# Keeping three quarters, not two, of one weight granule in PSUM, with attention sums and turned tiles in other banks

## The chip, the cores and the metric

One core of one Trainium2 chip runs the kernel. The metric is the device time of one execution in microseconds (us), lower being better. Three plain executions of the kernel before and one profiled execution are known.

## The reference

The reference normalises a bf16 sequence `x` of 2048 rows and 1024 columns and sends it through a recurrent attention layer with memory and through a layer that handles two routed rows. Cut to what matters here:

```
xn = layernorm(x)
mem = mem0                                  # 8 rows x 1024
for s in range(64):                         # segments of 32 rows
    h = concat(mem, xn[32*s : 32*s+32])     # 40 rows
    q, k, v = h @ Wq, h @ Wk, h @ Wv        # 32 heads x 128
    p = softmax(mask(q @ k.T / sqrt(128)))
    o = (p @ v) @ Wo                        # 40 x 1024
    mem = o[:8]                             # carried on
    outs.append(o[8:])
y = gate/up/down on the two rows of xn with the largest xn @ w_r
out = x + concat(outs) + xn, plus y * sigmoid(r) added at the two rows
```

Every segment needs the memory that the one before it made, so the 64 segments run one after the other, and each of them uses all four weight matrices (32 MiB in bf16).

## The kernel before

**Weights.** The matrices are cut into 64 granules of 128 partitions by 2048 bf16 columns, 512 KiB each: granules 0 to 47 are the halves of Wq, Wk and Wv in the order of the six phases (eight granules to a phase: q first half, k first half, q second half, k second half, v first half, v second half), and 48 to 63 are Wo. Of these, 44 stay in SBUF for the whole run. The other 20 (the list `STREAMED`) are used in every segment and are streamed: `fetch` (L366) loads each into one of five slots of the pool `wstream` (tile `g`), from copies `wsc` in DRAM that segment 0 makes. A slot is reloaded when TensorE has used its granule for the last time in the segment; the load is issued by SP, whose queue is in program order, so the loads come in the order of use.

**What of the streamed granules stays in PSUM.** Two streamed granules are kept in PSUM too. Granule 6 (`KEPT_WHOLE`) is kept whole, in the tiles KEPT0 and KEPT1, and never loaded after segment 0; ScalarE and VectorE copy its four quarters (512 columns each) to SBUF in each segment (`bring_back`, L389). Of granule 25 (`KEPT_PART`, the second granule of the fourth phase) the last two quarters are kept, in KEPT2. In each segment from 1 on, `fetch` loads its first 1024 columns (256 KiB), and VectorE copies the other two quarters from KEPT2 into the same slot (`kept_piece`, L393). In segment 0, `keep` (L377 to L382) brings a quarter to PSUM: four transposes on TensorE into the tile BT, a copy to SBUF on VectorE (XK, L380), and four transposes back into the KEPT tile.

**A segment.** For a granule, TensorE makes four matmuls (L817) of the segment's 32 rows (24 new rows and 8 rows of memory, tile ST) into an accumulator PSm. The eight new rows that each segment leaves out of ST are gathered over four segments and projected for four segments at once (`left_pass`, L579, tile STL; `project_left`, L598). ScalarE empties the accumulators (XB, L836; VM, L846). Half a phase later, XB is turned by four transposes (L649) into BT and copied out as QT (ScalarE, L657) or KT (VectorE, L664); next to the first QT also the left rows LX are turned (L502) and copied as QKL (ScalarE, L506). Then follow the scores in the tile BS (L672, L674), the softmax on VectorE and ScalarE (L681 to L720), the attention sums (`attend`, L736 and L738), which are copied as OT and OTL (L745, L747), and the product with Wo (L586) into WO. In the midst of that product, at its ninth granule, the next segment's rows XN are turned (L301) and copied to the next ST (L315). The memory rows come last: X (L885), turned (L301) and copied to ST by VectorE (L324).

**Banks.** BS and BT are one PSUM bank each (128 partitions by 512 f32 columns). Before the change BT holds turned tiles in its first half (`PTB`) and, in its second half, the turned LX (`PTB2`) or half of the attention sums (`OPB`). BS holds the scores (columns 0 to 319), the other half of the sums of the second half of heads, and row statistics from column 320 on. The order of instructions is the one in which the code is written, with hooks at (phase, granule); waits are set between any two engines that use one bank, whichever columns they use.

Of the kernel before, what the change touches and what calls it, by code (L numbers as in the profile page):

```python
# [8 lines left out]
BF16 = mybir.dt.bfloat16  # L9
# [11 lines left out]
KEPT_PART = 25  # L21
# [29 lines left out]
def kernel(  # L51
# [16 lines left out]
    nc = tc.nc  # L68
# [9 lines left out]
    NT = S // P  # L78
# [6 lines left out]
    NK = M + SEG  # L85
# [43 lines left out]
    def columns(g, s):  # L129
        if s > 0 and g == KEPT_WHOLE:  # L130
            return None
        return slice(0, 1024 if s > 0 and g == KEPT_PART else 2048)

    wsc = {g: dram.tile([P, columns(g, 1).stop - columns(g, 1).start], BF16, name=f"wsc{g}")
           for g in streamed if g != KEPT_WHOLE}
# [24 lines left out]
    BS = psS.tile([P, 512], F32, name="BS")  # L160
    BT = psT.tile([P, 512], F32, name="BT")
    SPS = BS[:, 0:8 * NK].rearrange("p (i a k) -> p i a k", i=4, a=2)
    PTB = BT[:, 0:256].bitcast(BF16)
    PTB2 = BT[:, 256:512].bitcast(BF16)
    OPB = BT[:, 256:256 + 4 * NK]
    MR = BS[:, 320:320 + 2 * NSEG].rearrange("p (s c) -> p s c", c=2)
    ML = BS[:, 448:448 + 2 * NT].rearrange("p (t c) -> p t c", c=2)
    MLR = BS[:, 480:480 + 2 * NT].rearrange("p (t c) -> p t c", c=2)
# [30 lines left out]
    for s in range(4):  # L199
        nc.vector.tensor_copy(out=SELM[:, s, :, 0:XM],  # L200
                              in_=IDENT[:, 32 * s:32 * s + XM].unsqueeze(1).to_broadcast([P, 4, XM]))
        nc.vector.tensor_copy(out=SELL[:, s, :, :],
                              in_=IDENT.rearrange("p (s c) -> p s c", c=32)[:, :, XM:SEG])
        nc.vector.tensor_copy(out=SELR[:, s, :, :],
                              in_=IDENT.rearrange("p (s c) -> p c s", c=32)[:, XM:SEG, :])
# [78 lines left out]
    def norm_seg(s):  # L284

        x = X[s % 2]
        mr = two_rows(MR[:, s, :], "ri")
        ab = mr[:, 2:4]
        nc.vector.tensor_scalar(out=ab[:, 0:1], in0=mr[:, 1:2], scalar1=1.0, scalar2=KMSK, op0=ALU.add, op1=ALU.mult)
        nc.vector.tensor_scalar(out=ab[:, 1:2], in0=mr[:, 0:1], scalar1=mr[:, 1:2], scalar2=-1.0, op0=ALU.mult, op1=ALU.mult)  # L290
        xn = front.tile([P, 256], BF16, tag="st", name="XN")
        nc.vector.tensor_scalar(out=xn[:, :], in0=x[:, :], scalar1=mr[:, 0:1], scalar2=mr[:, 1:2],
                                op0=ALU.subtract, op1=ALU.mult)
        nc.vector.tensor_scalar(out=x[:, :], in0=x[:, :], scalar1=ab[:, 0:1], scalar2=ab[:, 1:2],
                                op0=ALU.mult, op1=ALU.add)
        return xn

    def turn(src, at=0):
        PTx = PTB[:, 256 * at:256 * (at + 1)].rearrange("p (c g r) -> p c g r", c=2, g=4)
        for c in range(2):  # L300
            nc.tensor.transpose(out=PTx[:, c, :, :].rearrange("p g r -> p (g r)"), in_=src[:, c * P:(c + 1) * P],  # L301
                                identity=IDENT[:, :])
        return PTx
# [1 line left out]
    def gview(st):  # L305
        return st.rearrange("p (g c) r -> p c g r", c=2)

    def turn_rows(xn, xl):

        return turn(xn), turn(xl, 1) if xl is not None else None  # L310

    def new_st(turned):
        PTx, PTl = turned
        st = front.tile([P, KC, SEG], BF16, tag="st", name="ST")
        nc.scalar.copy(out=gview(st)[:, :, :, 0:XM], in_=PTx[:, :, :, 0:XM])  # L315
        if PTl is None:
            return st, None
        stl = one.tile([P, KC, SEG], BF16, tag="stl", name="STL")
        nc.scalar.copy(out=gview(stl), in_=PTl[:, :, :, :])
        return st, stl  # L320

    def mem_to_st(OB, st):
        PTm = turn(OB)
# [17 lines left out]
    def sum_left(t, G):  # L341
# [10 lines left out]

    KEPT = [psK.tile([P, 1024], BF16, name=f"KEPT{b}") for b in range(3)]
    KEPT_COLS = {KEPT_WHOLE: {0: KEPT[0][:, 0:512], 1: KEPT[0][:, 512:1024], 2: KEPT[1][:, 0:512], 3: KEPT[1][:, 512:1024]},
                 KEPT_PART: {2: KEPT[2][:, 0:512], 3: KEPT[2][:, 512:1024]}}

    def fetch():
        if not flow:
# [14 lines left out]
    def keep(g, t):  # L373
        for c, K in KEPT_COLS[g].items():
            turned = PTB.rearrange("p (i r) -> p i r", i=4)
            for i in range(4):
                nc.tensor.transpose(out=turned[:, i, :], in_=t[:, 512 * c + P * i:512 * c + P * (i + 1)],  # L377
                                    identity=IDENT[:, :])
            XK = one.tile([P, 512], BF16, tag="vl0", name="XK")
            nc.vector.tensor_copy(out=XK[:, :], in_=PTB)  # L380
            for i in range(4):
                nc.tensor.transpose(out=K[:, P * i:P * (i + 1)], in_=XK[:, P * i:P * (i + 1)], identity=IDENT[:, :])  # L382

# [7 lines left out]
    def kept_piece(g, c, copy):  # L391
        t = [t for q, t in queued if q == g][0]
        copy(out=t[:, 512 * c:512 * (c + 1)], in_=KEPT_COLS[g][c])  # L393
# [30 lines left out]
    def granule(g):  # L424
        if g in res_tiles:
            return res_tiles[g]
        got, t = queued.pop(0)
        assert got == g, (got, g)
        return t
# [26 lines left out]
    row_stats(xt(0), S6, MV[:, 0, :])  # L456
    spread(0, 1)
    norm_left(XL0, 0)
    ST, STL = new_st(turn_rows(norm_seg(0), XL0))
    mem_to_st(OB, ST)  # L460

    side = {}
# [34 lines left out]
    lx = [None]  # L497

    def turn_lx():
        PTq = PTB2.rearrange("p (i c) -> p i c", i=4)  # L500
        for il in range(4):
            nc.tensor.transpose(out=PTq[:, il, :], in_=lx[0][:, il * P:(il + 1) * P], identity=IDENT[:, :])  # L502

    def new_qkl():
        t = qkl[0] = one.tile([P, 4, 4, 4, XL], BF16, tag="bC", name="QKL")
        nc.scalar.copy(out=t.rearrange("p i m q r -> p (i m q r)"), in_=PTB2)  # L506

    def turn_first(mat, half, XBl):
        if mat == 0 and half == 0:
# [122 lines left out]
    for s in range(NSEG):  # L632
# [10 lines left out]
        def hook(p, kc, fn):  # L643
            hooks.setdefault((p, kc), []).append(fn)
# [79 lines left out]
        def attend(half, ph, turn_too=None):  # L724
            if half not in sums:
                if half not in OT:
                    OT[half] = one.tile([P, 4, 4, SEG], BF16, tag=("kt", "bC")[half], name="OT")
                if half == 0:
                    nxt["wo"] = psA.tile([P, 512], F32, tag="acc", name="WO")
                sums[half] = [BS[:, 0:4 * NK] if half else nxt["wo"][:, 256:256 + 4 * NK], OPB]  # L730
            PTm, PTl = PTs[half]
            for il in range(4):
                for jl in range(2):
                    q0 = 32 * (2 * ph + jl)
                    o = sums[half][jl][:, il * NK:(il + 1) * NK]
                    nc.tensor.matmul(o, lhsT=VM[half][q0:q0 + 32, il * P:(il + 1) * P], rhs=PTm[q0:q0 + 32, il, 0:NK],  # L736
                                     start=True, stop=False, tile_position=(q0, 0), skip_group_check=True)
                    nc.tensor.matmul(o, lhsT=VL[half][q0:q0 + 32, il * P:(il + 1) * P], rhs=PTl[q0:q0 + 32, il, 0:NK],  # L738
                                     start=False, stop=True, tile_position=(q0, 0), skip_group_check=True)
            if turn_too is not None:  # L740
                turn_too()
            for jl in range(2):
                ov = sums[half][jl].rearrange("p (i q) -> p i q", i=4)
                copy = nc.scalar.copy if half == 0 or jl == 0 else nc.vector.tensor_copy
                copy(out=OT[half][:, 2 * ph + jl, :, :], in_=ov[:, :, 0:SEG])  # L745
                h0 = 16 * half + 8 * ph + 4 * jl
                copy(out=left_out()[:, h0:h0 + 4, j, :], in_=ov[:, :, SEG:NK])  # L747
# [42 lines left out]
        if s > 0:  # L790
            hook(0, 0, lambda: bring_back(3, nc.scalar.copy))
            hook(0, 1, lambda: bring_back(0, nc.vector.tensor_copy))
            hook(2, 1, lambda: kept_piece(KEPT_PART, 2, nc.vector.tensor_copy))
            hook(2, 2, lambda: kept_piece(KEPT_PART, 3, nc.vector.tensor_copy))
        hook(2, 6, lambda: scores(0))
        hook(3, 4, exponent)
        hook(3, 4, lambda: soften(0))
# [54 lines left out]
        assert not hooks, hooks  # L852

        WO = nxt["wo"]
        if s + 1 < NSEG:
            xn = norm_seg(s + 1)
            left_too = nxt["xl"] if j == 0 and G + 1 < NT else None
            turned = []

        def lhs_main(h):  # L860
# [3 lines left out]
        for w in range(16):  # L864
            if w == 5:
                attend(1, 0)
            if w == 8 and s + 1 < NSEG:
                attend(1, 1, lambda: turned.append(turn_rows(xn, left_too)))
                nxt["st"], stl = new_st(turned[0])
                STL = stl or STL  # L870
            elif w == 8:
                attend(1, 1)
            Gv = granule(48 + w)
            project(WO, w, Gv, lhs_main, w == 15, first=(w == 0))
            held[48 + w] = Gv
            run_passes(6, w)
            if w == 9 and s + 1 < NSEG:
                new_lx(s + 1)
                bring_back(1, nc.scalar.copy)
                bring_back(2, nc.vector.tensor_copy)  # L880
            if w == 11 and j == 3:
                xl_of[0] = load_left(G, one.tile([P, 256], BF16, tag="stl", name="OL")[:, :], True)
            release(6, w)
# [129 lines left out]
```

## Time and profile before

| what | value |
|---|---|
| three executions | 1874.32, 1879.33, 1879.33 us (median 1879.33) |
| the profiled execution's own time | 1871.24 us |
| its span, first to last instruction | 1869.5 us |
| PE busy, DVE busy, ACT busy, POOL busy | 84%, 47%, 37%, 24% of the span |
| moved by DMA | 712.27 MB, mean 381 GB/s |
| granted TensorE clock, mean | 0.956 |

PE is TensorE's matmul row, PEld its weight loads, DVE VectorE, ACT ScalarE, POOL GpSimd and SP the engine that issues the loads. In the groups of instructions a row is: line, engine, operation, out<-in, shapes, count, then busy time, mean ns of one, and idle time before them with what ended it. In the waits a row is: who waited, for whom, us in total, times, longest. In the table by stretches the last two columns are the mean busy share of the 16 DMA engines (packets overlap a little, so that it can pass 1.00) and GB/s. Segment 0, with the first loads of all weights, takes the time up to about 131 us; the last segment begins at about 1784 us.

### The profile page before, as it was taken

The page shows a single profiled execution, that of the slowest core. Times are in us where ns is not written, and L with a number is a line of the kernel's source. Part 1 is how long each engine was busy: PE and PEld are TensorE (multiplying, and loading weights), DVE is VectorE, ACT ScalarE, POOL GpSimd, SP SyncE. Part 2 cuts the span into 40 slices and gives each one's busy share as a digit, 9 for nine tenths or more (in the row PEclk, how much of TensorE's full clock was granted, in tenths as well). Part 3 has the DMA queues.
Part 4 walks back from the last instruction along what each step waited for, and adds up shares of the span by engine and source line. Part 5 has one row for each costly group of instructions (what it writes and reads, how often), then busy time and mean ns, then how long its engine had stood idle before and what let it go on. Part 6 is the DMA issues. An engine that isn't in the chain of part 4 may idle for free.

```text
span 1869.5 us, 80499 instructions
## 1 busy us (share of the span) xinstructions
PE 1565.6 (84%) x34978; PEld 851.4 (46%) x34978; DVE 886.3 (47%) x2935; ACT 692.7 (37%) x1948; POOL 455.8 (24%) x898
## 2 busy tenths in 40 slices
PE   3458998898888989988899889988898888888764
PEld 1124444444454544444445444444444444444433
DVE  6725544544454454444444454444544454445430
ACT  1113433444343334433443344433433343434320
POOL 3211322213131321323132221323132121312120
PEclk8669999999999999999999999999999999999995
DMA  9999999999999999999999999999999999999998
GB/s 371 399 358 391 382 367 391 390 370 369 379 381 379 376 374 388 382 390 373 388 384 400 379 391 385 379 398 375 392 368 382 380 385 390 379 395 380 374 403 325
DMA packets 232115, 712.27 MB, mean 381 GB/s; under 512 B 39040, under 2 KB 52912, under 8 KB 231760
## 3 DMA queue, kind: packets, MB, share of 16 engines
q1 hardware_dynamic: 194384, 671.18, 93.0%
q0 software_dynamic: 28736, 28.08, 4.7%
q10 hardware_dynamic: 8640, 7.87, 1.2%
q8 instruction: 274, 4.49, 0.9%
q14 instruction: 81, 0.66, 0.1%
HBM read 694.32 MB, written 22.29 MB: 383 GB/s over the span
## 4 chain that ended last, share of the span: by engine, by line
DMA 58%; PE 35%; DVE 4%; issue 2%; SPq 1%; ACT 1%; POOL 0%; DVEq 0%; POOLq 0%; ACTq 0%
DMA g<-wsc 50%; PE PSm L817 18%; PE WO L586 5%; PE PSl L579 4%; PE BT L649 2%; DMA XP<-in_A_x_dram 2%; PE WL L598 2%; DMA MW<-in_B_w_up_dram 1%; DVE XR L256 1%; DMA MW<-in_B_w_gate_dram 1%; DMA g<-in_A_Wq_dram 1%; DMA wres<-in_A_Wo_dram 1%; DMA g<-in_B_w_down_dram 1%; PE BT L301 1%; DMA out_dram<-X 1%
## 5 line engine op out<-in xcount | busy, mean ns | idle before, releaser
L817 PE MATMUL PSm<-wres,ST 128*32 128x512 bf16 x8448 | 702.2, 383 | 9.1 <-DMA wres<-in_A_Wv_dram 4.1
L817 PEld LDWEIGHTS <-ST 128*32 128x32 bf16 x12288 | 322.4, 96 | 411.2 <-issue 163.8
L817 PE MATMUL PSm<-g,ST 128*32 128x512 bf16 x3588 | 359.8, 385 | 100.0 <-DMA g<-wsc 77.0
L586 PEld LDWEIGHTS <-OT 128*32 128x32 bf16 x8192 | 219.9, 98 | 157.3 <-issue 130.5
L836 ACT CAST XB<-PSm 128x512 bf16<-128x512 f32 x256 | 150.5, 588 | 283.8 <-PE PSm L817 281.3
L586 PE MATMUL WO<-wres,OT 128*32 128x256 bf16 x5632 | 240.8, 281 | 13.9 <-DMA wres<-in_A_Wo_dram 7.5
L495 POOL DMA_DIRECT2D LX<-ql_d x63 | 35.3, 560 | 819.6 <-PE WO L586 380.6
L586 PE MATMUL WO<-g,OT 128*32 128x256 bf16 x2560 | 133.8, 283 | 76.5 <-DMA g<-wsc 66.3
L579 PE MATMUL PSl<-wres,STL 128*32 128x512 bf16 x2112 | 185.9, 390 | 1.6 <-issue 1.5
L664 DVE COPY KT<-BT 128x512 bf16<-128x512 bf16 x112 | 45.8, 409 | 290.7 <-issue 177.4
L887 POOL DMA_DIRECT2D out_dram<-X x256 | 129.8, 514 | 199.6 <-DVE X L885 158.6
L281 POOL DMA_DIRECT2D X<-in_A_x_dram x256 | 129.7, 513 | 188.3 <-PE PSm L817 88.7
L657 ACT COPY QT<-BT 128x512 bf16<-128x512 bf16 x128 | 75.0, 586 | 125.4 <-PE BT L502 73.6
L389 ACT COPY BK<-KEPT 128x512 bf16<-128x512 bf16 x126 | 74.4, 590 | 120.7 <-PE WO L586 93.2
L649 PEld LDWEIGHTS <-XB 128*128 128x128 bf16 x1024 | 58.4, 98 | 117.1 <-ACT XB L836 65.5
L579 PEld LDWEIGHTS <-STL 128*32 128x32 bf16 x3072 | 84.5, 98 | 57.3 <-issue 11.9
L649 PE MATMUL BT<-IDENT,XB 128*128 128x128 bf16 x1024 | 101.8, 222 | 8.7 <-ACT XB L836 7.3
L846 ACT CAST VM<-PSm 128x512 bf16<-128x512 f32 x128 | 76.0, 594 | 84.4 <-PE PSm L817 82.9
L736 PEld LDWEIGHTS <-VM 32*128 32x128 bf16 x2048 | 66.4, 91 | 84.8 <-issue 70.0
L885 DVE TENSOR_TENSOR X<-WO,X 128x256 bf16<-128x256 f32 x64 | 27.1, 424 | 160.9 <-PE WO L586 160.9
L745 DVE CAST OT<-BT 128x128 bf16<-128x128 f32 x128 | 37.2, 291 | 126.7 <-PE BT L301 71.6
L745 ACT CAST OT<-BS 128x128 bf16<-128x128 f32 x128 | 34.1, 266 | 166.0 <-PE BT L738 89.7
(175 smaller groups left out, 2406.9 us busy)
## 6 DMA issues: line engine op xcount, KB each, us to landing
g<-wsc SPq DMA_DIRECT2D x1134, 512.0 KB, 6.1
g<-wsc SPq DMA_DIRECT2D x63, 256.0 KB, 5.6
LX<-ql_d POOLq DMA_DIRECT2D x63, 128.0 KB, 5.8
ql_d<-XBl ACTq DMA_DIRECT2D x60, 128.0 KB, 5.8
MW<-in_B_w_gate_dram SPq DMA_DIRECT2D x16, 448.0 KB, 9.1
MW<-in_B_w_up_dram SPq DMA_DIRECT2D x16, 448.0 KB, 9.4
wres<-in_A_Wk_dram SPq DMA_DIRECT2D x12, 512.0 KB, 11.9
MW<-in_B_w_down_dram SPq DMA_DIRECT2D x12, 512.0 KB, 10.5
```

What stands on the lines that cost most here:

```text
L281: nc.gpsimd.dma_start(out=X[s % 2][32 * g:32 * g + XM, :], in_=x2[s * SEG:s * SEG + XM, 256 * g:256 * (g + 1)])
L389: copy(out=back[c][:, :], in_=KEPT_COLS[KEPT_WHOLE][c])
L579: nc.tensor.matmul(PSl[32 * jq:32 * jq + 32, :], lhsT=STL[:, g % KC, :], rhs=part(Gv, jq), start=first_, stop=last_, tile_position=(0, 32 ...
L586: nc.tensor.matmul(PS[32 * g:32 * g + 32, 0:256], lhsT=lhs(h), rhs=Gv[:, D * hs + 256 * g:D * hs + 256 * (g + 1)], start=(first and hs == ...
L649: nc.tensor.transpose(out=PTq[:, il, :, :].rearrange("p j r -> p (j r)"), in_=XB[:, il * P:(il + 1) * P], identity=IDENT[:, :])
L657: nc.scalar.copy(out=QT[half][:, :, :], in_=pv)
L736: nc.tensor.matmul(o, lhsT=VM[half][q0:q0 + 32, il * P:(il + 1) * P], rhs=PTm[q0:q0 + 32, il, 0:NK], start=True, stop=False, tile_position ...
L745: copy(out=OT[half][:, 2 * ph + jl, :, :], in_=ov[:, :, 0:SEG])
L817: nc.tensor.matmul(PSm[32 * jq:32 * jq + 32, :], lhsT=ST[:, kc, :], rhs=part(Gv, jq), start=(kc == 0), stop=(kc == KC - 1), tile_position= ...
L836: nc.scalar.copy(out=XB[:, :], in_=PSm[:, :])
L846: nc.scalar.copy(out=VM[half][:, :], in_=PSm[:, :])
L887: nc.gpsimd.dma_start(out=out2[s * SEG:s * SEG + XM, 256 * g:256 * (g + 1)], in_=OB[32 * g:32 * g + XM, :])
```

## The change

Three of granule 25's quarters are kept, and the load of that granule in segments 1 to 63 shrinks from 256 to 128 KiB (1024 bytes of each partition). The third quarter lies in BT's second half, so what lay there moves: the sums `OPB` to BT's first half, the turned LX to BS (`PTS`), and the turned XN to columns 160 to 287 of BS. The left rows of the next group (`left_too`, one segment in four) are turned into BT on their own, at the thirteenth granule of Wo rather than the ninth. `kept_piece` runs three times per segment, at hooks (2, 0) to (2, 2), and XK in segment 0 is copied by ScalarE.

```diff
-        return slice(0, 1024 if s > 0 and g == KEPT_PART else 2048)
+        return slice(0, 512 if s > 0 and g == KEPT_PART else 2048)
...
-    PTB2 = BT[:, 256:512].bitcast(BF16)
-    OPB = BT[:, 256:256 + 4 * NK]
+    PTS = BS[:, 0:256].bitcast(BF16)
+    OPB = BT[:, 0:4 * NK]
...
-                 KEPT_PART: {2: KEPT[2][:, 0:512], 3: KEPT[2][:, 512:1024]}}
+                 KEPT_PART: {1: BT[:, 256:512].bitcast(BF16), 2: KEPT[2][:, 0:512], 3: KEPT[2][:, 512:1024]}}
...
-            nc.vector.tensor_copy(out=XK[:, :], in_=PTB)
+            nc.scalar.copy(out=XK[:, :], in_=PTB)
...
-        PTq = PTB2.rearrange("p (i c) -> p i c", i=4)
+        PTq = PTS.rearrange("p (i c) -> p i c", i=4)
...
-        nc.scalar.copy(out=t.rearrange("p i m q r -> p (i m q r)"), in_=PTB2)
+        nc.scalar.copy(out=t.rearrange("p i m q r -> p (i m q r)"), in_=PTS)
...
-            hook(2, 1, lambda: kept_piece(KEPT_PART, 2, nc.vector.tensor_copy))
-            hook(2, 2, lambda: kept_piece(KEPT_PART, 3, nc.vector.tensor_copy))
+            for c in range(1, 4):
+                hook(2, c - 1, lambda c=c: kept_piece(KEPT_PART, c, nc.vector.tensor_copy))
...
             if w == 8 and s + 1 < NSEG:
-                attend(1, 1, lambda: turned.append(turn_rows(xn, left_too)))
-                nxt["st"], stl = new_st(turned[0])
-                STL = stl or STL
+                attend(1, 1, lambda: turned.append(turn(xn, BS[:, 160:288].bitcast(BF16))))
+                nxt["st"] = new_st(turned[0])
             elif w == 8:
                 attend(1, 1)
+            if w == 12 and left_too is not None:
+                STL = new_stl(turn(left_too))
```

Line numbers of the changed kernel are two to four lower from L301 on (L393 becomes L389, L389 becomes L385, L657 becomes L654).

The first place where the order of work changes is VectorE's queue early in a segment. These are its rows in the 26th segment after segment 0, before the change (a row is line, operation, out<-in, shape, and the semaphores that it waits for by engine or DMA queue):

```order
L324 COPY ST<-BT 128x2x4x8 [waits PE_49,Activation_49]
L389 COPY BK<-KEPT_193 128x512 [waits DMAHW4_49,Activation_49]
L393 COPY g<-KEPT_195 128x512 [waits DMAHW6_49,DMAHW7_49,DMAHW1_49,PE_49]
L393 COPY g<-KEPT_195 128x512
L664 COPY KT<-BT 128x16x32 [waits DVE_49,PE_49,Activation_49]
L681 TENSOR_TENSOR BS<-BS,CT 128x4x24 [waits PE_49]
```

The same place with the change:

```order
L320 COPY ST<-BT 128x2x4x8 [waits PE_49]
L385 COPY BK<-KEPT_193 128x512 [waits DMAHW4_49,Activation_49]
L389 COPY g<-BT 128x512 [waits DMAHW6_49,DMAHW7_49,DMAHW1_49,Activation_49]
L389 COPY g<-KEPT_195 128x512 x2
L661 COPY KT<-BT 128x16x32 [waits DVE_49,PE_49,Activation_49]
L678 TENSOR_TENSOR BS<-BS,CT 128x4x24 [waits PE_49]
```

There are three kept copies where there were two. The first reads BT and waits for ScalarE, whose last use of BT before it is the copy QT of the segment's first phase, where the first of the two waited for TensorE's last use of the slot. VectorE's next instruction is still the copy KT.

The second place is ScalarE's queue from the last attention sums of one segment to the copies QT and QKL of the next. Before the change:

```order
L745 CAST OT<-BS 128x128 [waits PE_49]
L747 CAST OTL<-BS 128x4x8
L315 COPY ST<-BT 128x2x4x24 [waits DVE_49,PE_49]
L389 COPY BK<-KEPT_193 128x512
L389 COPY BK<-KEPT_194 128x512 [waits DVE_49,PE_49,Activation_49]
L836 CAST XB<-PSm 128x512 [waits PE_49,Activation_49]
L657 COPY QT<-BT 128x512 [waits DVE_49,PE_49,Activation_49]
L506 COPY QKL<-BT 128x512
```

With the change:

```order
L742 CAST OT<-BS 128x128 [waits PE_49]
L744 CAST OTL<-BS 128x4x8
L310 COPY ST<-BS 128x2x4x24 [waits DVE_49]
L385 COPY BK<-KEPT_193 128x512
L385 COPY BK<-KEPT_194 128x512 [waits DVE_49,PE_49,Activation_49]
L833 CAST XB<-PSm 128x512 [waits PE_49,Activation_49]
L654 COPY QT<-BT 128x512 [waits DVE_49,PE_49,Activation_49]
L503 COPY QKL<-BS 128x512 [waits PE_49]
```

The instructions and their order are the same. ST and QKL are now read from BS, and QKL has a wait on TensorE of its own: QT waits for the transposes of XB alone, QKL for those of LX.

More of the change, by code (lines that the diff above doesn't have):

```diff
@@ L296, in norm_seg, with turn @@
         return xn
[L298 to L299 removed]
+    def turn(src, to=PTB[:, 0:256]):
+        PTx = to.rearrange("p (c g r) -> p c g r", c=2, g=4)
         for c in range(2):
@@ L306, in gview, with new_st, new_stl @@
         return st.rearrange("p (g c) r -> p c g r", c=2)
[L308 to L313, printed above, removed]
+    def new_st(PTx):
         st = front.tile([P, KC, SEG], BF16, tag="st", name="ST")
         nc.scalar.copy(out=gview(st)[:, :, :, 0:XM], in_=PTx[:, :, :, 0:XM])
-        if PTl is None:
-            return st, None
+        return st
+    def new_stl(PTl):
         stl = one.tile([P, KC, SEG], BF16, tag="stl", name="STL")
         nc.scalar.copy(out=gview(stl), in_=PTl[:, :, :, :])
-        return st, stl
+        return stl
     def mem_to_st(OB, st):
@@ L458 @@
     norm_left(XL0, 0)
-    ST, STL = new_st(turn_rows(norm_seg(0), XL0))
+    ST = new_st(turn(norm_seg(0), PTS[:, 0:256]))
+    STL = new_stl(turn(XL0))
     mem_to_st(OB, ST)
@@ L854 @@
         WO = nxt["wo"]
+        left_too = nxt["xl"] if j == 0 and G + 1 < NT else None
         if s + 1 < NSEG:
             xn = norm_seg(s + 1)
-            left_too = nxt["xl"] if j == 0 and G + 1 < NT else None
             turned = []
```

## The prediction

> **What bounds the kernel now.** I read the DMA side first, because the change removes bytes. The table by stretches (us; PE, PEld, DVE, ACT and POOL busy with counts; granted clock; DMA share; GB/s) for start, segments and end:
>
> ```profile
> 0.00:120.00 120.00, 51.59 (x679) 23.74 (x680) 77.53 (x199) 16.04 (x41) 27.79 (x64) 0.72 1.01 390
> 120.00:1809.00 1689.00, 1492.33 (x33726) 811.80 (x33729) 802.50 (x2711) 671.43 (x1899) 420.70 (x821) 0.99 1.00 382
> 1809.00:1870.00 61.00, 21.66 (x581) 15.90 (x573) 6.23 (x25) 5.21 (x8) 7.30 (x13) 0.54 0.89 340
> ```
>
> Over the 1689 us of the segments the 16 DMA engines are busy for a share of 1.00, while PE is busy for 1492 of 1689 us, 88%. So the transfers are the first suspect. The waits say whether PE feels it, and how SP's loads are held:
>
> ```profile
> PE PSm L817 <- DMA g<-wsc: 77.0, 167, 2.0
> PE WO L586 <- DMA g<-wsc: 66.3, 135, 1.7
> SPq L366 <- PE PSm L817: 434.9, 652, 3.5
> ```
>
> PE stands 143.3 us in 302 waits for streamed granules, out of 1197 loads, 2.27 us per segment over 63 segments. It is not idle everywhere, though: SP waits far longer for PE to give a slot back (434.9 us and more) than PE waits for loads. Five slots tie the two together, and the chain that ended last has both in it:
>
> ```profile
> DMA 58%; PE 35%; DVE 4%; issue 2%; SPq 1%; ACT 1%; POOL 0%; DVEq 0%; POOLq 0%; ACTq 0%
> DMA g<-wsc 50%; PE PSm L817 18%; PE WO L586 5%; PE PSl L579 4%; PE BT L649 2%; DMA XP<-in_A_x_dram 2%; PE WL L598 2%; DMA MW<-in_B_w_up_dram 1%; DVE XR L256 1%; DMA MW<-in_B_w_gate_dram 1%; DMA g<-in_A_Wq_dram 1%; DMA wres<-in_A_Wo_dram 1%;
> ```
>
> Half of the span runs through streamed loads and 35% through PE. Where in a segment is which? Granule 25 is loaded and used some 5 to 10 us after a segment's start, so I took that stretch in eight segments that follow each other:
>
> ```profile
> 969.10:974.10 5.00, 5.00 (x116) 2.54 (x112) 2.90 (x11) 1.98 (x5) 1.74 (x4) 1.00 1.04 389
> 994.20:999.20 5.00, 5.00 (x116) 2.56 (x112) 2.14 (x6) 2.50 (x6) 1.63 (x4) 1.00 1.02 383
> 1020.00:1025.00 5.00, 5.00 (x120) 2.43 (x116) 2.15 (x7) 2.83 (x6) 1.91 (x4) 1.00 0.96 361
> 1045.90:1050.90 5.00, 4.62 (x108) 2.34 (x107) 2.14 (x6) 1.83 (x5) 2.01 (x4) 1.00 0.99 395
> 1073.60:1078.60 5.00, 4.67 (x108) 2.31 (x107) 2.90 (x11) 1.98 (x5) 2.05 (x4) 1.00 1.02 381
> 1099.10:1104.10 5.00, 4.71 (x108) 2.33 (x107) 2.14 (x6) 2.50 (x6) 2.00 (x4) 1.00 1.00 392
> 1125.90:1130.90 5.00, 5.00 (x116) 2.46 (x112) 2.14 (x6) 2.85 (x6) 2.00 (x4) 1.00 0.95 342
> 1151.70:1156.70 5.00, 4.92 (x112) 2.37 (x108) 2.14 (x6) 2.12 (x6) 1.50 (x3) 1.00 0.99 362
> ```
>
> Here PE is busy for 38.9 of 40 us, and the DMA share is below its full value (1.04 in the first row) in most segments: 0.95 and 0.96 in two of them. In this stretch PE sets the pace and the queue of loads is nearly, not always, full. Later in the segment PE waits, as the 66.3 us at WO show. The bytes are thus taken away just where transfers bind least, which is why I don't take the whole saving.
>
> **The change part by part.** *The load.* What one row of a transfer costs is read from the queues: packets, MB, and the share of 16 engines' span, of which 1869.5 us x 16 = 29,912 us is all.
>
> ```profile
> q1 hardware_dynamic: 194384, 671.18, 93.0%
> q10 hardware_dynamic: 8640, 7.87, 1.2%
> g<-wsc SPq DMA_DIRECT2D x1134, 512.0 KB, 6.1
> g<-wsc SPq DMA_DIRECT2D x63, 256.0 KB, 5.6
> ql_d<-XBl ACTq DMA_DIRECT2D x60, 128.0 KB, 5.8
> ```
>
> SP's queue q1 spends 0.930 x 29,912 / 671.18 = 41.4 engine-us per MB, with rows of 3.5 KB on the mean; ACT's q10, the 128 KB stores with 1 KB to a partition, spends 0.012 x 29,912 / 7.87 = 45.6. The new load has the shape of the latter: 0.131 MB x 45.6 / 16 = 0.37 us of all engines. The old one, 0.262 MB, lies between 41.4 and 45.6 per MB, 0.68 to 0.75 us. The saving is 0.30 to 0.37 us per segment; from the landings (6.1 against 5.6 us for 256 KB less, halved) it would be 0.25. Over 63 segments that makes 16 to 23.5 us of DMA time. I take 0.31 us, 19.5 us in all, near the lower end of the queue's bounds, since 2 KB rows are nearer to q1's.
>
> *What of it reaches the end.* Two readings. First, room in the stretch above: (1.04 - share) x 5 us is 0, 0.10, 0.40, 0.25, 0.10, 0.20, 0.45, 0.25 us; of 0.31 us there is left, where the room is smaller, 0.31, 0.21, 0, 0.06, 0.21, 0.11, 0 and 0.06, a mean of 0.12, or 39%. That is too harsh, since part of the idle time lies ahead of granule 25's own transfer or on single engines only. Second, the whole segment: PE waits 2.27 us of it, and the engines fall short of 1.04 by 0.04 x 26.6 us = 1.06 us (62 segments between about 131 and 1784 us, some 26.6 each); if time follows each side in proportion to the other side's idling, DMA counts for 2.27 / (2.27 + 1.06) = 68%. I take 60% of 19.5 us, nearer to the second: 12 us. The bounds are 39% of 16 us (6 us) and all of 23.5 us.
>
> *The third kept copy* costs VectorE 63 x 0.42 us = 26 us at 47% busy. It matters only where VectorE is waited for. The rows and one segment's timeline (start, us, what):
>
> ```profile
> L393 DVE COPY g<-KEPT 128x512 bf16<-128x512 bf16 x126 | 47.5, 419 | 95.2 <-PE PSm L817 51.4 <-DMA g<-wsc 25.1 <-PE PSl L579 18.7
> 1018.80 0.59 ACT L657 COPY QT<-BT 128x512 bf16<-128x512 bf16 x1 [1.21 <-PE BT L502]
> 1021.41 0.42 DVE L664 COPY KT<-BT 128x512 bf16<-128x512 bf16 x1 [4.14 <-ACT XBl L627]
> ```
>
> The three copies now stand behind QT: from 1018.80 + 0.59 = 1019.39 they would run to 1019.39 + 3 x 0.42 = 1020.65, and KT starts at 1021.41, 0.76 us later; granule 25 is used later still. VectorE stood idle for 4.14 us here, so the cover is its own idle time. Without that cover each further 0.1 us would delay the scores, and PE with them, by 6 us over 63 segments. Cost taken: 0.
>
> *QT, QKL and ST from other banks.* ScalarE's wait for LX ahead of QT goes:
>
> ```profile
> ACT QT L657 <- PE BT L502: 73.6, 63, 3.0
> 1018.16 0.33 PE BT L649 x4
> 1018.49 0.22 PE BT L502 x4
> ```
>
> QT can start 0.22 us sooner, which widens the 0.76 us to about 1 us; QKL ends when it did. Nothing of PE's waits for either: gain 0. At the ninth granule of Wo the wait changes hands:
>
> ```profile
> DVE OT L745 <- PE BT L301: 71.6, 63, 2.7
> 1014.40 0.22 PE BT L301 x2
> ```
>
> VectorE's copy of the sums waited for the two transposes of XN, because both lie in BT; now ScalarE's does, in BS. The later of the two is as late as before, and OT's consumer is four granules off: 0. The left rows, turned four granules later in 15 segments, must be copied before the passes after the last Wo granule; with some 0.2 us of PE per granule that is tight, and I bound it by 15 x 0.2 = 3 us, taking 0 (PE waits there for loads anyway).
>
> *Segment 0.* VectorE was late with XK; ScalarE, nearly idle there, is not, and one more quarter is brought over:
>
> ```profile
> PE KEPT L382 <- DVE XK L380: 10.3, 6, 5.6
> ```
>
> At most those 10.3 us of PE go, and about 2 us for the added quarter come; but the first 120 us are DMA-bound with PE busy for 52 of them, so between 0 and 8 us, taken at 0.5 (the copy to DRAM of one granule is 128 KB shorter).
>
> Sum: 12 + 0.5 = 12.5 us less than the profiled execution's 1871.24 us, 1859 us. That execution is 8 us below the median of the three others (1879.33); the four have a mean of 1876.1, and from there the time is 1864 us. A difference of 0.3%, 5.6 us, is about what a measurement of this kernel can tell from none.
>
> **The rivals.** *All of it arrives*: the loads bind after all, and 19.5 to 23.5 us go, with up to 3 us of segment 0: 1853 us. For it: share 1.00 over 1689 us; against: the share of 0.95 beside a PE without a gap.
>
> *It is hidden*: the slots are given back by PE, so a shorter transfer only makes the engines wait sooner, and PE's stretch is unchanged: 0 to 5 us, 1874 us. For it: the eight rows above; against: one of them is at 1.04, and the waits come later in the same segment.
>
> *VectorE becomes late* and the kernel slower. The three copies have to keep clear of ScalarE's and PE's use of BT; if QT is late by more than the 0.76 to 1 us found above, KT, the scores and PE's next transposes into BT wait behind them. With nothing hidden, 63 x 1.26 us = 79 us of PE; as PE holds 35% of the chain, 28 us, less the 12.5: 1891 us. It begins to decide when the trio starts over 1 us later after QT than its end. Against it: the 4.14 us of idle time ahead of KT. The Trainium skill speaks for this mechanism ("PSUM — Partial Sum Buffer", section "PSUM bank collisions raise a hardware error"): PSUM has to be guarded by bank and quadrant, not by address, so disjoint halves of BT don't run side by side. The trace agrees, in the 71.6 us above.
>
> **How the numbers follow.** The forecast (6 to 19 us less) gets 0.54, all of it 0.18, hidden 0.18, slower 0.10. Faster by over 0.3%: 0.54 + 0.18 = 0.72; within: 0.18; slower: 0.10. The range goes from 1850 us, all of it with something of segment 0, to 1876, the mean of the runs before, which leaves out the slower case and a little at the other end.
>
> **What would show it.** Right: q1 moves 8.3 MB less (63 x 0.131), PE's waits for `g<-wsc` fall from 143 us by about 12, the DMA share stays at about 1.00 but drops a little in the stretch 5 to 10 us after a segment's start, KT and the scores start no later in the segment, and QT waits for L646 alone. Wrong: waits of PE's scores on KT or of L646 on the kept copy; waits for loads that stay at 143 us with an unchanged span, which would mean that it is hidden; or a share that holds at 1.00 everywhere with 20 us gone.

## The result, and the profile after

| | before | after |
|---|---|---|
| median of 22 executions each, same chip | 1874.26 us | 1872.89 us |
| ratio after / before, 95% interval | | 1.0003 (0.9986 to 1.0021) |
| span of the profiled execution | 1869.5 us | 1868.9 us |
| moved by DMA | 712.27 MB | 703.88 MB |

No change that can be measured. The ratio compares the undisturbed executions (one of the 22 was disturbed on either side), so it isn't quite that of the two medians. Its lower end allows a gain of 0.0014 x 1871 = 2.6 us, where 12.5 were forecast.

The bytes are gone. On the page of the changed kernel, the totals and SP's queue (packets, MB, share of 16 engines), and the issues of the two kinds of load (count, size, median us from issue to landing):

```profile
DMA packets 232082, 703.88 MB, mean 377 GB/s; under 512 B 39040, under 2 KB 60976, under 8 KB 231728
q1 hardware_dynamic: 194384, 662.92, 92.7%
g<-wsc SPq DMA_DIRECT2D x1134, 512.0 KB, 6.0
g<-wsc SPq DMA_DIRECT2D x63, 128.0 KB, 5.2
```

671.18 - 662.92 = 8.26 MB, which is 63 x 131 KB. A quarter of the bytes of a full load lands in 5.2 us, the whole in 6.0. The time was not moved with the bytes. The stretch of the segments in the table by stretches, of after:

```profile
120.00:1809.00 1689.00, 1496.48 (x33724) 814.75 (x33727) 822.66 (x2771) 667.56 (x1897) 420.08 (x820) 0.99 1.00 377
```

The rate fell from 382 to 377 GB/s, by 1.3%, about the share of the saved bytes (8.39 of 712 MB), while the DMA share still reads 1.00. PE is as busy as before. The waits of after (who waited, for whom, us, times, longest):

```profile
PE WO L583 <- DMA g<-wsc: 68.8, 135, 1.5
PE PSm L814 <- DMA g<-wsc: 68.3, 149, 1.6
...
ACT OT L742 <- PE BS L301: 80.9, 63, 3.1
...
PEld L669 <- DVE KT L661: 25.9, 63, 1.1
```

PE's waits for loads went from 143.3 to 137.1 us (8.7 us less ahead of PSm, 2.5 more at Wo), half of the fall that was forecast, and nothing was gained at the end. The wait at Wo's ninth granule changed hands as foreseen (71.6 us on VectorE, now 80.9 on ScalarE), and the scores wait 25.9 us in all for KT, as before (25.8).

Where did the saving go? The same eight stretches as in the prediction, 5 to 10 us behind the start of eight segments that follow each other, in the changed kernel:

```profile
968.30:973.30 5.00, 4.89 (x108) 2.37 (x100) 3.31 (x14) 1.61 (x4) 3.01 (x6) 1.00 1.03 386
994.40:999.40 5.00, 4.79 (x112) 2.34 (x104) 3.00 (x9) 2.10 (x6) 1.79 (x4) 1.00 1.02 373
1020.30:1025.30 5.00, 5.00 (x118) 2.44 (x113) 2.65 (x8) 2.69 (x6) 2.00 (x4) 1.00 0.97 352
1045.70:1050.70 5.00, 5.00 (x116) 2.46 (x119) 2.31 (x8) 2.05 (x5) 2.01 (x4) 1.00 1.02 386
1071.60:1076.60 5.00, 5.00 (x120) 2.58 (x116) 3.56 (x14) 1.97 (x5) 2.62 (x6) 1.00 0.90 305
1100.60:1105.60 5.00, 4.98 (x116) 2.49 (x112) 3.23 (x9) 2.71 (x6) 2.00 (x4) 1.00 0.97 349
1127.00:1132.00 5.00, 4.67 (x108) 2.33 (x104) 2.49 (x8) 2.34 (x5) 1.80 (x4) 1.00 0.97 319
1153.50:1158.50 5.00, 4.77 (x108) 2.32 (x104) 2.86 (x9) 1.77 (x5) 2.01 (x4) 1.00 0.88 322
```

The mean share was 1.00 and is 0.97; the mean rate was 376 GB/s and is 349. PE is busy for 39.1 of 40 us, as it was (38.9). Summed from all packets of the trace by the time they ended, the MB in each 5 us behind a segment's start are (means over 60 segments, standard errors 0.01 to 0.02):

| us behind the start | 0 to 5 | 5 to 10 | 10 to 15 | 15 to 20 | 20 to 25 |
|---|---|---|---|---|---|
| before | 1.941 | 1.809 | 1.936 | 1.966 | 1.927 |
| after | 1.937 | 1.716 | 1.891 | 1.977 | 1.927 |

From 5 to 15 us 0.138 MB are missing, the 0.131 MB of the saving, and no other load was brought forward to fill the place. A load can't be: it starts when PE gives its slot back. So the engines simply moved less there. Over all segments, granule 25 landed 1.32 us ahead of its first matmul (0.93 before; 33 loads of each trace have a landing on record), granules 29, 33 and 36 by 0.38, 0.27 and 0.12 us further ahead than before, and granule 42, at 15 us, 0.06 us ahead (0.07 before). The slots were refilled at the same times: counted from a segment's start, each of the 19 loads is issued within 0.13 us of when it was before, on the mean. The mean segment took 26.65 us in both.

### The profile page after: what moved, and what is told of

Read it like the earlier page. It is cut to its first block, busy times and chain, and to the rows that moved or that the text cites. A ratio compares the mean times of both kernels' runs of the same rounds, so it can differ in the third digit from the quotient of the medians.

```text
span 1868.9 us, 80531 instructions
## 1 busy us (share of the span) xinstructions
PE 1572.4 (84%) x34986; PEld 854.2 (46%) x34986; DVE 905.0 (48%) x2992; ACT 693.7 (37%) x1955; POOL 455.9 (24%) x898
## 2 busy tenths in 40 slices
DMA packets 232082, 703.88 MB, mean 377 GB/s; under 512 B 39040, under 2 KB 60976, under 8 KB 231728
## 3 DMA queue, kind: packets, MB, share of 16 engines
q1 hardware_dynamic: 194384, 662.92, 92.7%
## 4 chain that ended last, share of the span: by engine, by line
DMA 58%; PE 37%; DVE 1%; issue 1%; ACT 1%; SPq 1%; POOL 0%; ACTq 0%; DVEq 0%
DMA g<-wsc 48%; PE PSm L814 19%; PE WO L583 5%; PE PSl L576 5%; PE BT L646 3%; DMA XP<-in_A_x_dram 2%; PE WL L595 1%; DMA MW<-in_B_w_gate_dram 1%; DMA g<-in_A_Wv_dram 1%; DMA MW<-in_B_w_up_dram 1%; DMA g<-in_A_Wq_dram 1%; DMA g<-in_A_Wk_dram 1%; DMA wres<-in_A_Wv_dram 1%; DMA wres<-in_A_Wo_dram 1%; SPq L145 1%
## 5 line engine op out<-in xcount | busy, mean ns | idle before, releaser
L814 PEld LDWEIGHTS <-ST 128*32 128x32 bf16 x12288 | 327.4, 96 | 406.7 <-issue 178.1
L389 DVE COPY g<-BT 128x512 bf16<-128x512 bf16 x63 | 26.7, 424 | 285.8 <-ACT QT L654 237.0
L385 ACT COPY BK<-KEPT 128x512 bf16<-128x512 bf16 x126 | 75.8, 602 | 120.4 <-PE WO L583 120.4
L654 ACT COPY QT<-BT 128x512 bf16<-128x512 bf16 x128 | 74.9, 585 | 109.0 <-PE BT L646 103.6
L883 DVE TENSOR_TENSOR X<-WO,X 128x256 bf16<-128x256 f32 x64 | 27.2, 424 | 175.8 <-PE WO L583 175.8
L678 DVE TENSOR_TENSOR BS<-BS,CT 128x96 f32<-128x96 f32 (+1 forms) x256 | 59.1, 231 | 73.4 <-PE BS L671 68.8
```

The source lines that it names most:

```text
L385: copy(out=back[c][:, :], in_=KEPT_COLS[KEPT_WHOLE][c])
L654: nc.scalar.copy(out=QT[half][:, :, :], in_=pv)
L678: nc.vector.tensor_tensor(out=S4, in0=S4, in1=m, op=ALU.add)
L814: nc.tensor.matmul(PSm[32 * jq:32 * jq + 32, :], lhsT=ST[:, kc, :], rhs=part(Gv, jq), start=(kc == 0), stop=(kc == KC - 1), tile_position= ...
```

## Experiments

Unless it is said otherwise an experiment starts from the kernel before, and a gain is what its ratio lacks to 1, times 1871 us. The prediction's 0.31 us of all engines for 128 KiB, 19.5 us in 63 segments, is called full price.

### Apart: the bytes alone, the moves alone

*bytes_alone* leaves banks and copies as they were and shortens only the load.

```diff
-        return slice(0, 1024 if s > 0 and g == KEPT_PART else 2048)
+        return slice(0, 512 if s > 0 and g == KEPT_PART else 2048)
...
```

> The kernel before with 128 KiB less of granule 25 per segment; nothing moves in PSUM, two kept copies as before, and the matmuls of the second quarter read the first one, so the output is not the reference's. Paced by PE (the transfer is shortened in a stretch where PE sets the pace, the engines only wait sooner): within 5 us of before. Offset (the bytes pay 12 to 20 us and the moves in PSUM cost as much): 12 to 20 us faster. Transfers never bind: no change.

*moves_alone* is the changed kernel with the load and the kept copies of before.

```diff
-        return slice(0, 512 if s > 0 and g == KEPT_PART else 2048)
+        return slice(0, 1024 if s > 0 and g == KEPT_PART else 2048)
...
-            for c in range(1, 4):
+            for c in range(2, 4):
                 hook(2, c - 1, lambda c=c: kept_piece(KEPT_PART, c, nc.vector.tensor_copy))
```

> The changed kernel with the load of granule 25 back at 256 KiB and two kept copies: the moves in PSUM and the later turn of the left rows alone. Paced by PE: within 5 us of before. Offset: 12 to 20 us slower. Transfers never bind: no change.

Measured: bytes_alone 1.0015 (0.9989 to 1.0041), moves_alone 1.0016 (0.9989 to 1.0043). Neither can be told from no change, so it isn't that a real gain was eaten by the moves: the bytes alone give at most 2 us.

### More bytes less, early and late

*early_whole* drops granule 25's load altogether, *late_half* half of granule 50's, where PE does wait for loads; both are 256 KiB less per segment.

```diff
-            nc.sync.dma_start(out=t[:, c], in_=wsc[g][:, :])
+            if g == KEPT_PART:
+                short[id(t)] = (t, [2, 3, 2, 3])
+            else:
+                nc.sync.dma_start(out=t[:, c], in_=wsc[g][:, :])
...
```

> The kernel before without any load of granule 25 after segment 0: 256 KiB less per segment, 0.62 to 0.75 us of DMA time, 39 to 47 us in all; its slot is still taken and the matmuls of the first two quarters read the two kept ones, so the output is not the reference's. Paced by PE: 0 to 12 us faster, the load time turning into engines that wait 5 to 14 us after a segment's start. Offset: 24 to 47 us faster. Transfers never bind: no change.

```diff
+LESS = {50: 1024}
...
-            nc.sync.dma_start(out=t[:, c], in_=wsc[g][:, :])
+            c = slice(0, LESS.get(g, c.stop))
...
+            nc.sync.dma_start(out=t[:, c], in_=wsc[g][:, c])
...
```

> The kernel before with half of granule 50 (a Wo granule, used 19 us after a segment's start, where PE waits for loads) not loaded after segment 0: the same 256 KiB less per segment as in early_whole, only later; the other half is read twice, so the output is not the reference's. Paced by PE: 20 to 40 us faster, PE's waits for streamed granules at WO falling by about as much. Offset: as early_whole. Transfers never bind: no change.

Measured: early_whole 0.9967 (0.9942 to 0.9992), 6 us less; late_half 0.9977 (0.9951 to 1.0003), 4 us less. Full price would be 39 us in both. My theory of that moment, that PE sets the pace early and the loads late, fell with late_half.

### PE's work, early and late

Twelve matmuls more per segment, 0.65 us of PE or 41 us in all, at granule 16 (*pe_early*) or granule 40 (*pe_late*).

```diff
+                for jq in list(range(4)) * (3 if s > 0 and (p, kc) == (2, 0) else 0):
+                    nc.tensor.matmul(PSm[32 * jq:32 * jq + 32, :], lhsT=ST[:, kc, :], rhs=part(Gv, jq),
+                                     start=True, stop=True, tile_position=(0, 32 * jq))
```

(pe_late has `(5, 0)` for `(2, 0)`.)

> The kernel before with twelve matmuls more per segment from 1 on, at the first granule of the third phase (about 5 us after a segment's start): three extra rounds of that granule's four, overwritten by the real ones. At 0.22 us per four that is 0.65 us per segment, 41 us in all. If PE sets the pace there: 30 to 41 us slower. If the DMA engines' rate binds: 0 to 10 us. If the loop of five slots binds (a slot is given back later, so each load starts later): 15 to 41 us, here and late alike.

> The same twelve matmuls at the first granule of the sixth phase, about 14 us after a segment's start, where PE waits for most streamed granules. If PE sets the pace early and transfers set it late: 0 to 15 us slower, PE's waits for loads falling by as much as is hidden. If the DMA engines' rate binds: 0 to 10 us. If PE's work binds everywhere: 30 to 41 us.

Measured: 1.0124 (1.0072 to 1.0176), 23 of the 41 us, and 1.002 (0.9989 to 1.0052), 4 of them. PE's work does count in the early part, where granule 25 lies, and hardly in the late part. Neither side has its full price anywhere.

### The number of slots

```diff
-N_SLOT = 5
+N_SLOT = 4
```

> The kernel before with four slots instead of five. If the time from issue to landing (6 us, of which most would be fixed) times the number of loads is what binds: 19 loads x (5.1 + 0.9) us / 4 slots = 28.5 us per segment against 26.6, 120 us slower or more. If the DMA engines' rate or PE binds: 0 to 40 us slower.

For *slots6* (and, the same kernel once more, *slots6_again*; on the changed kernel *slots6_after*) the room comes from granule 15:

```diff
-N_SLOT = 5
+N_SLOT = 6
...
+        if g == 15:
+            res_tiles[15] = res_tiles[14]
+            return
```

> The kernel before with six slots; for their room granule 15 is not stored and granule 14's tile is read in its place, so the output is not the reference's and one 512 KiB load of segment 0 falls away (about 1 us). If the loop of slots binds: 20 to 60 us faster, PE's waits for streamed granules falling from 143 us by as much. If the DMA engines' rate or PE binds: within 8 us of before.

Measured: four slots 1.117 (1.1096 to 1.1245), 219 us more; six slots 0.9581 (0.9539 to 0.9624), 78 us less, with all but the same bytes to move (711.75 for 712.27 MB) and 38 us of PE's waits for loads where 143 were. The waits of *slots4*:

```profile
PE PSm L817 <- DMA g<-wsc: 201.5, 308, 2.3
PE WO L586 <- DMA g<-wsc: 130.3, 186, 3.0
```

Loads land sooner (5.5 us for 6.1), and yet PE waits for them 332 us for 143: too few are under way. The next four set the change itself beside six slots, and make the room of the sixth by streaming granule 15 too (*six_own_before*, *six_own_after*):

```diff
-N_RES = 44
-N_SLOT = 5
+N_RES = 43
+N_SLOT = 6
...
-STREAMED = [2, 5, 6, 9, 13, 17,
+STREAMED = [2, 5, 6, 9, 13, 15, 17,
```

> The kernel before with a sixth slot; granule 15 is not stored and its matmuls read granule 14's tile, so the output is not the reference's. It is the measure for the next one. Loop of slots: 1794 us again, 77 us below the kernel before.

> The changed kernel (three quarters kept) with the same sixth slot and the same stand-in for granule 15, so the output is not the reference's. Loop of slots: with six slots PE waits only 38 us for loads, PE's own work sets the pace, and the saved 128 KiB have even less to give: 0 to 5 us below the six slots with two quarters (ratio to the kernel before 0.956 to 0.959). Rate of the DMA engines: at 401 GB/s the engines would now be the nearer to their limit, and the saved 63 x 0.31 us = 19.5 us would show at last, all of it or the larger part: 12 to 19 us below (ratio 0.948 to 0.952).

> The kernel before with a sixth slot whose room comes from streaming granule 15 as well (43 granules stored, 21 streamed, nothing left out): 20 loads per segment, 33 MB more in all. Loop of slots: 20 loads over six slots at a turn of 7.0 to 7.5 us are 23.3 to 25 us per segment, below the 25.4 us that PE's own pace gave with six slots, so nearly as fast as that: 1795 to 1820 us. Rate of the DMA engines: a segment moves 26.65 us x 382 GB/s = 10.2 MB and 0.52 MB more with it; at 382 GB/s that is 28.0 us (1956 us), at the 401 GB/s of the six slots 26.7 us (1870 us, no gain).

> The same sixth slot and 21 streamed granules in the changed kernel (three quarters kept, nothing left out). Loop of slots: 1795 to 1820 us, within 5 us of the two-quarter version with the same slots. Rate of the DMA engines: 19.5 us below that version, 1850 us at 401 GB/s and more at 382.

| | ratio to the kernel before | 95% interval |
|---|---|---|
| slots6_again | 0.9603 | 0.9564 to 0.9642 |
| slots6_after | 0.9559 | 0.9520 to 0.9598 |
| six_own_before | 0.9997 | 0.9968 to 1.0025 |
| six_own_after | 0.9976 | 0.9945 to 1.0007 |

With six slots the saved 128 KiB give 8 us by the ratios, with 21 streamed granules 4 us. Set directly against each other (same chip, six and twelve executions of each), the two of a pair differ by 8.5 us (95% interval 2.8 to 14.2) and by 3.3 us (-1.7 to 8.3). So with six slots there is a gain, with 21 granules none that can be told from nothing, and the full 19.5 us come in neither. The loop of slots was too simple a theory: it expected 1795 to 1820 us of six_own_before, and 1870.13 came out, just the time that the rate theory gave at 401 GB/s. But that theory also expected 19.5 us of six_own_after, so it isn't shown either. The rows of six_own_before (the table by stretches, the waits of PE, then one of SP's):

```profile
200.00:1600.00 1400.00, 1254.30 (x28394) 682.12 (x28390) 673.16 (x2285) 564.80 (x1599) 362.85 (x707) 1.00 1.02 404
```

```profile
PE PSm L817 <- DMA g<-wsc: 66.8, 141, 2.2
...
PE WO L586 <- DMA g<-wsc: 38.0, 93, 1.1
```

```profile
SPq L366 <- DMA ql_d<-XBl: 105.8, 56, 3.5
```

One load more per segment costs 71 us against slots6_again (1870.13 - 1799.53), over four fifths of its price of 63 x 0.524 MB x 41.4 / 16 = 85 us by q1's engine time per MB. That fits engines that are nearly full at 404 GB/s.

The last of these rows is a rival that neither theory counted. SP's loads and ACT's stores of XBl signal the same eight semaphores in turn, and SP, whose queue is in order, holds a load back until a store that had its semaphore before it has landed. Once in six_own_before, for instance, a store issued at 911.16 us landed at 917.73, and SP stood from 915.70 to 917.75 before the load that shares its semaphore. These waits were 2.4 us before, 65.7 in slots6_again, 18.4 in slots6_after, 105.8 in six_own_before and 107.0 in six_own_after. How much of the 71 us, and of the 8.5 us, is theirs no run separates. Together:

| run | slots | loads per segment | segment, us | mean landing, us | under way | DMA share | GB/s |
|---|---|---|---|---|---|---|---|
| slots4 | 4 | 19 | 30.18 | 5.56 | 3.5 | 0.95 | 337 |
| before | 5 | 19 | 26.65 | 6.09 | 4.3 | 1.00 | 382 |
| slots6_again | 6 | 19 | 25.56 | 6.69 | 5.0 | 1.02 | 399 |
| six_own_before | 6 | 20 | 26.49 | 6.84 | 5.2 | 1.02 | 404 |

(Segment and landing are means over the trace, share and rate those of 200 to 1600 us; under way = loads per segment x landing / segment.) The rate climbs with the number of loads under way, and more slowly towards 404, the most of these runs. The kernel before stands 5% below that; a sixth slot with the same loads takes it to 399.

### The price of bytes by place and by dose

Eight loads without their last quarter: *thin_lead* takes eight that land ahead of their use, *thin_bind* eight that land when PE already waits, and *thin_all* all eighteen full ones. *bytes_more* adds 256 KiB next to granule 25, outside the slots.

```diff
+THIN = [2, 5, 13, 21, 29, 33, 36, 56]
...
-            nc.sync.dma_start(out=t[:, c], in_=wsc[g][:, :])
+            c = slice(0, 1536) if g in THIN else c
+            nc.sync.dma_start(out=t[:, c], in_=wsc[g][:, c])
...
```

```diff
+    more_d = [dram.tile([P, 1024], BF16, name=f"more_d{b}") for b in range(2)]
...
             nc.sync.dma_start(out=t[:, c], in_=wsc[g][:, :])
+            if g == KEPT_PART:
+                nc.scalar.dma_start(out=more_d[s % 2][:, :], in_=wsc[29][:, 0:1024])
```

> The kernel before; eight streamed granules that land ahead of their use (2, 5, 13, 21, 29, 33, 36, 56; median lead 0.18 to 1.1 us) are loaded without their last quarter in segments 1 to 63, and the matmuls of that quarter read the third one, so the output is not the reference's: 63 x 8 x 128 KiB = 66 MB less, 9.3%. Loads that bind by their place: these bind seldom, 15 to 25 us less (ratio 0.987 to 0.992). A common rate of the engines: 8 x 19.5 = 156 us at full price, bounded by PE to about 80 us as with six slots (ratio 0.958), and in any case the same as thin_bind.

> The same with eight granules that land when PE already waits for them (9, 17, 42, 45, 47, 50, 59, 62; median lead 0.04 us), the same 66 MB less; the matmuls of the last quarter read the third one, so the output is not the reference's. Loads that bind by their place: 30 to 50 us less (ratio 0.973 to 0.984), about twice thin_lead; not all of 8 x 0.4 us x 63 = 200 us, since PE's own pace takes over. A common rate of the engines: as thin_lead.

> The kernel before; after the load of granule 25 in segments 1 to 63 ScalarE's queue copies another 256 KiB from DRAM to DRAM, which nobody reads (16.5 MB more, nothing left out). Loads that bind by their place: loads near it land a little later, which their lead of 0.4 to 1 us takes up: 0 to 10 us more (ratio 1.000 to 1.005). A common rate of the engines: 63 x 0.62 = 39 us more (ratio 1.021).

> The kernel before; all eighteen full loads of a segment (segments 1 to 63) without their last quarter, whose matmuls read the third one, so the output is not the reference's: 63 x 18 x 128 KiB = 149 MB less, 21%. At the price of 4.6 to 5.9 us per 128 KiB: 83 to 106 us less, 1765 to 1787 us; PE's own pace (1794 us with six slots, where it waited 38 us for loads) bounds it at about 1760. If the engines' rate bound for a part of a segment, its part would be gone after the first eight, and thin_all would give hardly more than them: 1810 to 1820 us.

| | 128 KiB per segment | ratio, 95% interval | us | us per 128 KiB (full: 19.5) |
|---|---|---|---|---|
| the change | -1 | 1.0003 (0.9986 to 1.0021) | +0.6 | none (up to 2.6) |
| early_whole | -2 | 0.9967 (0.9942 to 0.9992) | -6 | 3 |
| late_half | -2 | 0.9977 (0.9951 to 1.0003) | -4 | 2 |
| bytes_more | +2 | 1.0048 (1.0022 to 1.0073) | +9 | 4.5 |
| thin_lead | -8 | 0.9807 (0.9764 to 0.9850) | -36 | 4.5 |
| thin_bind | -8 | 0.9749 (0.9710 to 0.9789) | -47 | 5.9 |
| thin_all | -18 | 0.9315 (0.9272 to 0.9359) | -128 | 7.1 |

In this table a byte is paid at no more than 7.1 / 19.5 = 36% of the engines' time for it. Place matters less than I thought: thin_bind was to gain twice as much as thin_lead, and directly compared it is 9.6 us faster (0.1 to 19.1). The dose matters more: the two eights add up to 83 us, all eighteen give 128. The smaller doses are too uncertain to be ranked. The landings of thin_all, and its stretch:

```profile
g<-wsc SPq DMA_DIRECT2D x1134, 384.0 KB, 4.9
```

```profile
200.00:1600.00 1400.00, 1312.96 (x30535) 727.53 (x30526) 723.45 (x2458) 604.88 (x1716) 392.23 (x761) 1.00 0.95 318
```

With every load shorter, every slot turns sooner (4.9 us to landing for 6.1), and PE comes to 94% busy in this stretch (89% before). With one load shorter, the eighteen others keep their turns (6.0 for 6.1), and PE meets the next one of them as late as ever. That is an argument that fits the rows; a price that grows for another reason isn't excluded. My bound of 1760 us for PE's own pace in the expectation was wrong: 1742.08 us were measured.

### Shorter turns without fewer bytes

*halves* issues each full load as two of 1024 columns, each waiting for its own half of the slot.

```diff
+    slots = [wstream.tile([P, 2048], BF16, tag=f"g{b}", name="g") for b in range(N_SLOT)]
...
-            nc.sync.dma_start(out=t[:, c], in_=wsc[g][:, :])
+            for c0 in range(0, c.stop, 1024):
+                nc.sync.dma_start(out=t[:, c0:c0 + 1024], in_=wsc[g][:, c0:c0 + 1024])
```

> The kernel before with the five slots as fixed tiles and each full load issued as two loads of 1024 columns, each of which waits only for the matmuls that read its own half (the same bytes, twice the issues, rows of 2 KB for 4 KB; nothing left out). A turn of a slot sets the pace: half of each slot is refilled some 0.2 to 0.6 us sooner and lands sooner (5.6 for 6.1 us), 4 to 8% of a turn of 7.0 us: 30 to 77 us less (ratio 0.96 to 0.985). Time by packets and bytes in the engines: 144,000 packets more; with the 45.6 against 41.4 engine-us per MB of short and long rows 5 to 10% more DMA time in the loads, 30 to 100 us more (ratio 1.015 to 1.05).

Measured: 1.0569 (1.0517 to 1.0620), 106 us more. SP's own waits in it, and the landings:

```profile
SPq L374 <- DMA g<-wsc: 422.9, 1108, 2.0
SPq L374 <- PE PSm L825: 199.3, 448, 2.1
```

```profile
g<-wsc SPq DMA_DIRECT2D x2331, 256.0 KB, 5.4
```

SP now waits for landings (422.9 us for loads, 93.7 for stores) about as long as for PE (some 500 us in all); before it was 377.4 us for loads and some 840 for PE. In the trace each of the 2331 halves waits until the last transfer on its own semaphore has landed, where 65 of the 1197 loads before did. There are eight semaphores, so of ten half slots at most eight can be under way. On the mean 37 x 5.51 / 28.52 = 7.1 are, 3.6 granules' worth for 4.3 before, and the time lies between four and five slots accordingly. The share is 1.00 at 357 GB/s over 200 to 1680 us. It does not tell the two theories of its expectation apart: it ran into a limit that neither named, and rows got shorter at once. That shorter turns alone would pay stays untried.

## Why the prediction was wrong

- **The load's size was right.** Median times of SP's packets in the traces are 46, 84, 121 and 159 ns for rows of 1, 2, 3 and 4 KB. From 2 to 1 KB that is 38 ns x 128 rows / 16 engines = 0.30 us, against 0.31 taken. The landing did fall, from 5.6 to 5.2 us.
- **The step that failed is "what of it reaches the end"**, 60% of 19.5 us = 12 us. Measured is none, with 2.6 us as the bound, 13%. Both readings behind it, 39% from the room in the stretch and 68% from idle time on either side, took it that engine time set free is used by another transfer. The table of MB shows that it isn't: 0.138 MB are missing from 5 to 15 us, and nothing follows them, since the next loads wait for slots and are issued when they were before. That the measured 1872.89 us lies within the 1850 to 1876 us of the prediction is luck: the range ended at the mean of the runs before.
- **The first reading under it was wrong too:** the DMA share of 1.00 as "the first suspect" and 1.04 as full. At the same share of 1.00 the engines moved 382 GB/s before, 377 after and 357 in halves, and at 1.02 they moved 404. They had about 5% to spare. The second suspect, that SP waits far longer for PE than PE for loads, stood in the prediction and was the better guide.
- **The third copy, QT, QKL, ST and OT at 0:** right within the noise. The moves without the third copy (moves_alone) are at 1.0016, with it and the shorter load (the change) at 1.0003, and the scores' wait for KT is 25.9 us in the row above. The rival in which VectorE becomes late did not come: the first kept copy of after waits for QT, and does so in time that VectorE has:

```profile
L389 DVE COPY g<-BT 128x512 bf16<-128x512 bf16 x63 | 26.7, 424 | 285.8 <-ACT QT L654 237.0
```

- **Segment 0 at 0.5 us:** too small to be seen. PE's wait for XK is gone as foreseen for the most part (4.3 us ahead of KEPT and 0.7 ahead of BT, 10.3 before).

- **The rival "it is hidden"** named the outcome (0 to 5 us) and its mechanism, slots given back by PE and engines that wait sooner, and had 0.18. Of the eight rows that it cited, two (0.96 and 0.95) showed a share under 1 beside a PE without a gap, so the rows alone did not decide; SP's long waits for PE spoke for it too. What it had not: late in the segment, where PE waits, a byte hardly pays either (late_half). What stays open is how much of the low price is PE's pace, and how much the other loads' turns.

No complete kernel beat both by more than can be told; the nearest is six_own_after at 0.9976 (0.9945 to 1.0007). Six slots without a further streamed granule give some 4%, but a slot is 4 KB of each partition, as much as a stored granule, and the runs with six slots gave one up for it.

## What to carry to other kernels

Where transfers come through a ring of buffers, ask first what starts the next transfer. If it is a buffer given back, as here, a shorter transfer can free engine time that no other transfer uses, and one shorter transfer is then worth little. Count the transfers under way (number per turn x time to landing / turn) and see what one buffer more does, before bytes are traded for work on other engines. Look too for what else holds a transfer back, such as a semaphore that it shares with another.

## What the hardware showed that I had not expected

- **The DMA share is made of recorded packet times, and these stretch.** A 4 KB row of SP's queue takes 159 ns at the median in every trace here, but on the mean 162.9 ns in six_own_before (404 GB/s), 168.5 before (382), 169.8 after (377) and 180.4 in slots4 (337). The 3 KB rows of thin_all take 121 ns at the median and 143.8 on the mean, at 318 GB/s. The lower the rate, the longer the mean, which fits a recorded time that is in part waiting; that reading is argued, not shown. What the rows do show is that a share of 1.00 goes with 357 as with 382 GB/s, so a share near 1.00 does not tell a full engine.

- **A row costs little beyond its bytes.** The four medians lie on 8.5 ns + 0.0367 ns per byte, 27.2 GB/s for one engine and 436 for sixteen. The Trainium skill ("DMA: Bandwidth & Descriptors", section "Where 436 GB/s comes from") gives that as the ceiling, and the medians agree. The same section names about 358 GB/s as what binds between HBM and SBUF; the loads here come from DRAM, and 404 GB/s over 1400 us of six_own_before are above that, so here the measurement decides.
- **Landing is mostly not bytes.** Under the same load of the queue 128 KB land in 5.2 us and 512 KB in 6.0, and 512 KB in 5.5 us with four slots, 6.1 with five and 6.8 with six.
